# Banded attention joined to the MLP, with the tile scheduler choosing each engine's order

## The chip, the cores and the metric

The kernel runs on one core of one Trainium2 chip. The metric is the device time of the whole program in microseconds (us); most executions of a kernel agree within 0.3%. The core has five engines that matter here: PE (matrix products), ACT (table functions such as Exp, Ln and Sin), DVE (vector work), POOL (vector work, and the issue of DMAs that change the data type) and SP (other DMAs; ACT issues a few at the start). Each has its own queue of instructions. In the traces of this case an instruction waits behind those in front of it in its queue, also when its data are ready (POOL's copies between 95 and 120 us, below), and the waits between engines are read from semaphore events. The kernel is written in a tile language: the source gives the operations, and a scheduler decides in which order each engine's queue holds them, unless the source fixes it.

## The reference

```python
# 8 batches, 8 heads, 576 positions, head size 64; window 32; 8 global positions
scores = scale * q @ k.T
mask   = (|i - j| <= 32) | is_global[i] | is_global[j]
attn   = softmax(where(mask, scores, -1e9))
x      = (attn @ v), heads side by side              # 4608 tokens x 512
h      = x @ w_in                                    # 512 -> 2048
g      = h + sin(alpha * h)**2 / alpha
out    = g @ w_out                                   # 2048 -> 512
```

## The kernel before

The kernel before does dense attention for all batches, then the MLP. For each head it computes all 576 x 576 scores, transposed (keys on partitions), in six tiles of 96 keys, takes Exp on ACT, multiplies by a 0/1 mask on DVE, and multiplies by V with a column of ones appended, so that the softmax sum comes out as one more column.

```python
for b in range(B):
    if b == max(B - 2, 0):
        weight_prep()                # w_inp = w_in * alpha, w_outp = w_out / alpha, on DVE
    QS, KS, VS = ...                 # loads
    for hp in range(NHP):            # head pairs: transposes of q and k on PE, copies on DVE
        ...
        for t in range(2):
            for g in range(NKG):
                for gi in range(GK):
                    nc.tensor.matmul(out=scm[:, gi, :], lhsT=kTh[...], rhs=qTh[:, 0:SM], ...)
                    nc.tensor.matmul(out=sct[:, gi, :], lhsT=kTh[...], rhs=qTh[:, SM:S], ...)
                nc.scalar.activation(out=E[...], in_=scm[:, :, :], func=AF.Exp, scale=scale)
                nc.scalar.activation(out=E[...], in_=sct[:, :, :], func=AF.Exp, scale=scale)
                nc.vector.tensor_tensor(out=E[...], in0=E[...], in1=MASK[...], op=ALU.mult)
            ...                      # avq = E.T @ [V, 1]: 30 small matmuls; reciprocal, multiply on DVE
for tci in range(NCHUNK):            # 9 chunks of 512 tokens
    for nt in range(NT):             # 16: h2 = w_inp.T @ xT; Sb = Sin(h2) on ACT;
        ...                          # S2 = Sb*Sb and H2b = h2 + S2 on DVE
    ...                              # ops = H2b.T @ w_outp: 4 x 16 matmuls; copy on ACT; store
# (cut: set-up of the mask, transposes back, stores)
```

The softmax here doesn't subtract the row's maximum and nothing guards it: scores larger than these inputs give would overflow.

## Time and profile before

| | us |
|---|---|
| time, median | 733.14 |
| start, PE nearly idle | 0 to 81 |
| dense attention | 81 to about 471 |
| MLP, 28.2 us a chunk | about 475 to 732 |

Part 1 of the page (busy time of each engine and its share of the span), three rows of part 2 (busy share in 40 slices of the span, in tenths; PEclk is the clock granted to PE) and the first line of part 4 (the chain of work that ended last, by engine):

```profile
PE 642.0 (88%) x4360; PEld 352.6 (48%) x4384; DVE 412.0 (56%) x893; ACT 341.7 (47%) x566; POOL 107.7 (15%) x144
PE   0000699999999999999999999999999999999997
DMA  9999264918993999559968000001101001001001
PEclk9999999999999999999999999999999999999999
PE 83%; issue 6%; DVE 3%; POOL 3%; DMA 2%; ACT 2%; DVEq 0%; ACTq 0%; POOLq 0%
```

While the DMA engines bring in the first batch and the weights (DMA 9 in slices 1 to 4), PE does nothing for four slices; then it is full to the end, at full clock, and it makes up 83% of the chain. So PE sets the time, and the start stands in front of it. The costliest groups, part 5 (line, engine, operation, output<-inputs, shapes, count, busy us and mean ns of one, idle time before it and what ended it):

```profile
L259 PE MATMUL scm<-qT,kT 64*96 64x512 bf16 x384 | 202.2, 646 | 2.0 <-ACT E L273 0.9
L273 ACT ACTIVATE E<-scm 96x1024 bf16<-96x1024 f32 x192 | 195.8, 1020 | 41.1 <-PE scm L259 35.8
L285 DVE TENSOR_TENSOR E<-E,MASK 96x1152 bf16<-96x1152 bf16 x192 | 143.2, 747 | 24.9 <-ACT E L279 24.7
L297 PE MATMUL avq<-VS,E 96*128 96x65 bf16 (+1 forms) x1920 | 143.3, 245 | 1.1 <-DVE E L285 0.8
```

The first and last of these, 345 us of PE's 642, are dense scores and dense products with V. Three rows of the timeline of before matter for the argument, an early piece of DVE's work and the only two loads of function tables on ACT (start, duration, engine, line, and in brackets the idle time before and what ended it):

```profile
13.86 2.29 DVE L183 TENSOR_TENSOR w_inp<-wtmp,alphaB 128x2048 bf16<-128x2048 f32 x1 [3.75 <-DMA wtmp<-in_moe_w_in_dram]
...
81.55 1.28 ACT L273 ACT_TABLE_LOAD   x1 [81.55 <-PE sct L266]
...
474.77 1.28 ACT L369 ACT_TABLE_LOAD   x1 [3.72 <-issue]
```

The two loads bring in Exp's table and Sin's, each in 1.28 us. The first row shows DVE scaling `w_inp` at 14 us, although the source asks for it only before the seventh batch: the scheduler takes whatever is ready, from far ahead in the source.

### The profile page before, as it was taken

Reading aid. Unit: us, or ns where it says so; the run is one execution under the profiler, and the core shown is the slowest. Engines: PE = TensorE matmul, PEld = TensorE weight load, DVE = VectorE, ACT = ScalarE, POOL = GpSimd, SP = SyncE. Lnnn points to the kernel's source line nnn. Section 1 sums busy time; section 2 is a strip of 40 time slices with the busy share of each in tenths; the row PEclk is TensorE's granted clock in tenths of the full one; section 3 lists DMA queues with packets and bytes.
Section 4 is the critical chain, followed back from the end, with each engine's and each line's share of the span. In section 5 each row is a group of like instructions: output and inputs, shape, how many; then the busy total and the mean of one; then the engine's idle time right before and its main releaser. Section 6 shows DMA issues by size and latency. Waiting matters only on the chain.

```text
span 732.5 us, 10762 instructions
## 1 busy us (share of the span) xinstructions
PE 642.0 (88%) x4360; PEld 352.6 (48%) x4384; DVE 412.0 (56%) x893; ACT 341.7 (47%) x566; POOL 107.7 (15%) x144
## 2 busy tenths in 40 slices
PE   0000699999999999999999999999999999999997
PEld 0000356555665656565656666544444444444443
DVE  2466355555565655555555565594483573673762
ACT  0000465655565655555555565553353353353442
POOL 5167040122140131221500000000000000000000
PEclk9999999999999999999999999999999999999999
DMA  9999264918993999559968000001101001001001
GB/s 244 294 46 122 5 41 27 34 12 55 33 61 21 23 62 33 33 34 34 66 19 15 1 1 1 1 1 57 44 16 58 30 29 57 30 30 57 29 31 57
DMA packets 122529, 33.74 MB, mean 46 GB/s; under 512 B 115184, under 2 KB 115184, under 8 KB 121840
## 3 DMA queue, kind: packets, MB, share of 16 engines
q0 software_dynamic: 112256, 14.16, 49.3%
q1 hardware_dynamic: 10224, 18.89, 7.2%
q8 instruction: 34, 0.56, 0.3%
q14 instruction: 15, 0.12, 0.1%
HBM read 37.77 MB, written 9.44 MB: 64 GB/s over the span
## 4 chain that ended last, share of the span: by engine, by line
PE 83%; issue 6%; DVE 3%; POOL 3%; DMA 2%; ACT 2%; DVEq 0%; ACTq 0%; POOLq 0%
PE scm L259 21%; PE avq L297 17%; PE ops L383 17%; PE psx L237 5%; PE sct L266 5%; PE xps L329 2%; DMA QS<-in_q_dram 2%; DVE H2b L374 1%; ACT E L273 1%; POOL VS L79 1%; ACT Sb L369 1%; PE xps L335 1%; DVE Cq L111 1%; POOL KS L72 0%; POOL QS L72 0%
## 5 line engine op out<-in xcount | busy, mean ns | idle before, releaser
L273 ACT ACTIVATE E<-scm 96x1024 bf16<-96x1024 f32 x192 | 195.8, 1020 | 41.1 <-PE scm L259 35.8
L259 PE MATMUL scm<-qT,kT 64*96 64x512 bf16 x384 | 202.2, 646 | 2.0 <-ACT E L273 0.9
L285 DVE TENSOR_TENSOR E<-E,MASK 96x1152 bf16<-96x1152 bf16 x192 | 143.2, 747 | 24.9 <-ACT E L279 24.7
L297 PE MATMUL avq<-VS,E 96*128 96x65 bf16 (+1 forms) x1920 | 143.3, 245 | 1.1 <-DVE E L285 0.8
L297 PEld LDWEIGHTS <-E 96*128 96x128 bf16 (+1 forms) x1920 | 116.5, 135 | 53.1 <-issue 16.1
L383 PE MATMUL ops<-w_outp,H2b 128*128 128x512 bf16 x565 | 139.1, 379 | 0.6
L279 ACT ACTIVATE E<-sct 96x128 bf16<-96x128 f32 x192 | 51.8, 270 | 114.8 <-PE sct L266 114.4
L361 PEld LDWEIGHTS <-w_inp 128*128 128x128 bf16 x576 | 56.1, 98 | 74.3 <-issue 10.5
L383 PEld LDWEIGHTS <-H2b 128*128 128x128 bf16 x576 | 55.5, 98 | 68.8 <-DVE H2b L374 5.1
L266 PEld LDWEIGHTS <-kT 64*96 64x96 bf16 x384 | 58.4, 181 | 35.7 <-issue 26.7
L266 PE MATMUL sct<-qT,kT 64*96 64x64 bf16 x384 | 66.8, 264 | 0.0
L259 PEld LDWEIGHTS <-kT 64*96 64x96 bf16 x384 | 58.1, 173 | 15.3 <-issue 3.0
L391 ACT COPY osb<-ops 128x512 f32<-128x512 f32 x36 | 21.1, 585 | 84.3 <-PE ops L383 84.3
L237 PE MATMUL psx<-identb,QS 96*128 96x96 bf16 x192 | 21.9, 277 | 43.0 <-POOL identb masks.py:199 43.0
L237 PE MATMUL psx<-identb,KS 96*128 96x96 bf16 x192 | 26.2, 276 | 36.0 <-DVE qT L242 36.0
L305 DVE RECIPROCAL rec<-avq 128x4 f32<-128x4 f32 x64 | 11.7, 183 | 78.6 <-PE avq L297 78.6
L72 POOL DMA_DIRECT2D QS<-in_q_dram x48 | 36.9, 777 | 79.3 <-PE psx L237 78.5
L237 PEld LDWEIGHTS <-QS 96*128 96x128 bf16 x192 | 14.7, 133 | 57.2 <-issue 48.7
L237 PEld LDWEIGHTS <-KS 96*128 96x128 bf16 x192 | 15.4, 130 | 50.6 <-issue 50.6
L72 POOL DMA_DIRECT2D KS<-in_k_dram x48 | 36.9, 775 | 17.2 <-PE psx L237 15.1
L273 ACT ACT_TABLE_LOAD x1 | 1.3, 1283 | 81.5 <-PE sct L266 81.5
L242 DVE COPY kT<-psx 128x576 bf16<-128x576 bf16 x32 | 14.6, 455 | 33.0 <-PE psx L237 33.0
(614 smaller groups left out, 592.7 us busy)
## 6 DMA issues: line engine op xcount, KB each, us to landing
out_dram<-osb SPq DMA_DIRECT2D x36, 256.0 KB, 2.0
QS<-in_q_dram POOLq DMA_DIRECT2D x48, 96.0 KB, 3.6
KS<-in_k_dram POOLq DMA_DIRECT2D x48, 96.0 KB, 3.8
VS<-in_v_dram POOLq DMA_DIRECT2D x8, 576.0 KB, 11.1
wtmp<-in_moe_w_in_dram SPq DMA_DIRECT2D x4, 1024.0 KB, 8.4
alphaB<-in_moe_alpha_dram SPq DMA_DIRECT2D x1, 1024.0 KB, 5.8
wtmp_4073<-in_moe_w_out_dram SPq DMA_DIRECT2D x1, 1024.0 KB, 12.2
wtmp_4079<-in_moe_w_out_dram SPq DMA_DIRECT2D x1, 1024.0 KB, 10.4
```

The lines of the kernel that those rows point to most:

```text
L72: nc.gpsimd.dma_start(out=dstS[:, jt, :, :], in_=src[b, :, jt * KW : (jt + 1) * KW, :].rearrange("h p d -> p h d"),)
L237: nc.tensor.transpose(out=psx[:, jt * KW : (jt + 1) * KW], in_=srcS[:, jt, 2 * hp : 2 * hp + 2, :], identity=identb[0:KW, 0:KW],)
L259: nc.tensor.matmul(out=scm[:, gi, :], lhsT=kTh[:, k0 : k0 + KW], rhs=qTh[:, 0:SM], start=True, stop=True,)
L266: nc.tensor.matmul(out=sct[:, gi, :], lhsT=kTh[:, k0 : k0 + KW], rhs=qTh[:, SM:S], start=True, stop=True,)
L273: nc.scalar.activation(out=E[:, g * GK : (g + 1) * GK, 0:SM], in_=scm[:, :, :], func=AF.Exp, scale=scale,)
L279: nc.scalar.activation(out=E[:, g * GK : (g + 1) * GK, SM:S], in_=sct[:, :, :], func=AF.Exp, scale=scale,)
L285: nc.vector.tensor_tensor(out=E[:, g * GK : (g + 1) * GK, :], in0=E[:, g * GK : (g + 1) * GK, :], in1=MASK[0:KW, g * GK : (g + 1) * GK, :] ...
L297: nc.tensor.matmul(out=avq[0:qrows, qb, :], lhsT=E[:, kt, qs0 : qs0 + qrows], rhs=VS[:, hh * NKT + kt, :], start=(kt == 0), stop=(kt == NK ...
L329: nc.tensor.transpose(out=xps[:, qs0 : qs0 + QB], in_=xnp[:, qb, :], identity=identb[:, :],)
L361: nc.tensor.matmul(out=h2[:, :tn], lhsT=w_inp[:, c, nt * P : (nt + 1) * P], rhs=xT[:, c, t0 : t0 + tn], start=(c == 0), stop=(c == CT - 1),)
L383: nc.tensor.matmul(out=ops[:tsn, :], lhsT=H2b[:, nt, ts0 : ts0 + tsn], rhs=w_outp[:, nt, :], start=(nt == 0), stop=(nt == NT - 1),)
L391: nc.scalar.copy(out=osb[:tsn, :], in_=ops[:tsn, :])
```

## The change

The intent has three parts. First, only the band and the global rows and columns are computed: for 48 queries the keys are a window of 112 rows plus the 8 global ones, 120 of 128 partitions. A *unit* is one head pair and every second group of 48 queries; 8 units make a batch. Second, batch p's attention is emitted between matmuls of the MLP's second product for chunk p-1, and the first product of chunk p follows, so that PE has work while ACT and DVE do the softmax. Third, softmax's division is done on ACT as Exp(-Ln(den)). Work is also moved to POOL: 11 of the 16 squares of a chunk, half of `w_inp`'s scaling and all of `w_outp`'s.

```diff
+    MASK = const.tile([P, 2, NU, QC], BF, name="MASK")   # band and global rows
+    psA = tc.tile_pool(name="psA", bufs=1, space=PSUM)   # Sp, num, den, h2, ops, Kps: one buffer each
+    def stage_Q(b, hp, par):
+        Sp = psA.tile([P, 2, CH], F32, name="Sp")
+        for u in range(NU):                              # 6 matmuls, 112 columns each
+            nc.tensor.matmul(out=Sp[...], lhsT=kTw[hp][:, par, u, :], rhs=qBD[hp][:, par, u, :, :], ...)
+        nc.scalar.activation(out=E[:], in_=Sp[:, :, 0:EW], func=AF.Exp, scale=scale)
+        nc.vector.tensor_tensor(out=Ev, in0=Ev, in1=MASK[...], op=ALU.mult)
+    def stage_V(b, hp, par, E, xTb, gn, gd):
+        ...                                              # den = ones.T @ E (2), num = V.T @ E (6 matmuls)
+        nc.scalar.activation(out=lnd[:], in_=den[:], func=AF.Ln)
+        nc.scalar.activation(out=rec[:], in_=lnd[:], func=AF.Exp, scale=-1.0)
+        ...                                              # xTb = num * rec (2), gn = sum of num (2) on DVE
+        nc.vector.tensor_reduce(out=gd[:, par, hp, :], in_=den[:, :, QB:QC]..., op=ALU.add)
+    def stage_G(b, xTb, gn, gd):                         # global rows: 4 small DVE operations, then
+        for j in range(NG):
+            nc.gpsimd.tensor_copy(out=xTb[:, :, bass.ds(pregs[j], 1)], in_=xg[:, :, j : j + 1])
+        nc.vector.tensor_copy(out=xT[:, :, b * S : (b + 1) * S], in_=xTb[:])
+    # attention(b), before its first unit:
+                    nc.scalar.preload_act_table_set("natural_log_exp_and_others")
+    # first product of the MLP, squares shared between POOL and DVE:
+                nc.scalar.activation(out=Sb[:, 0:n, :], in_=h2[:], func=AF.Sin)
+                nc.gpsimd.tensor_tensor(out=S2[:, 0, :], in0=Sb[:, 0, :], in1=Sb[:, 0, :], op=ALU.mult)
+                if n == 2:
+                    nc.vector.tensor_tensor(out=S2[:, 1, :], in0=Sb[:, 1, :], in1=Sb[:, 1, :], op=ALU.mult)
+    # weights: w_inp half on DVE, half on POOL; w_outp on POOL
-    # (cut: dense scores, dense mask, the MLP as a phase of its own)
```

Nothing in the new source fixes the order on an engine. In particular the preload of the table set that holds both Ln and Exp has no data that it waits for.

## The prediction

> **What bounds the kernel now.** The busy table gives PE 642 of 732.5 us (88%), DVE 56%, ACT 47%, POOL 15%; the chain of waits is 83% PE. The timeline shows three stretches: about 81 us in which PE does nothing (loads, mask building), 390 us of dense attention (12.1 us per head pair, PE full), 257 us of MLP (28.2 us per chunk, PE full). Phases do not overlap; granted clock is 1.0.
>
> **What the change removes.** Dense scores become bands; most of the 202 us of scm and 143 us of avq matmuls goes. In the trace 26 avq matmuls with fresh weights take 1.68 us, 65 ns each, so a new unit (head pair, parity) costs 12 x 65 ns + 2 x 0.14 us, about 1.06 us; 64 units 68 us, transposes about 25 us. With the unchanged MLP (about 250 us) PE needs some 345 us. Estimates from the trace's shapes: ACT 225 us, DVE about 310 us, POOL 230 us. PE is no longer the sole limit.
>
> **What it adds and moves.** PSUM tiles Sp, num, den have one buffer each, so units run as a chain: matmuls 0.7 us, Ln 0.44, Exp 0.44 (from 96x1024 in 1.02, 96x128 in 0.27), two DVE multiplies 0.9 (128x256 took 0.42), three reduces 0.5, semaphore gaps 0.4: 3.4 us a unit, 27 us a batch, against 25 us of PE work there including the overlapped second MLP matmul. Then about 5 us of global rows and 18 us for the first MLP matmul. POOL squares are part of that: the Trainium skill, "GPSIMD Engine Reference", section 3.1, has tensor_tensor at 4497 ns for 128x2048; I estimate about 1.2 us for 512, 11 a chunk, equal to PE's 13.7 us. No trace shows it yet. Period about 53 us.
>
> **The scheduler.** In the trace of before, DVE scales weights at 14 us although the program asks for that at batch 6: order is chosen by readiness, far ahead. The preload of the combined Ln/Exp table has no data to wait for, so I expect all of them hoisted to the start. The Trainium skill, "ScalarE: Activation LUTs", section "Table sets", says one set holds both Ln and Exp; after Sin has evicted it, I expect separate Exp and Ln sets to be loaded in turn, two loads a unit. The trace has a load at 1.28 us (two of them, agreeing with that page's 1283 ns). Both sit in the unit's chain: 3.4 becomes 5.8 us, and the period about 71 us. I give this two chances in three.
>
> **Sum.** Start 50, batch 0 about 32, first MLP 18, seven periods, tail 45. Without thrashing 516 us, with it 642 us. Point 590, range 470 to 690. Faster 0.90, within 2% 0.04, slower 0.06. The removed PE work lies wholly on today's critical path.
>
> **What would show it.** ACT table loads: about 120 (thrash) or about 18. PE busy near 350 us, with its idle time waiting on DVE (num, den released) in attention and on POOL or DVE in the MLP. First score matmul near 50 us. POOL squares about 1.2 us.
>
> **What would make it wrong.** The scheduler keeps preloads in place (then about 500). Exp of the next batch mixed among Sins gives still more loads. POOL or DMA bound: q, k, v packets kept the DMA about 80% busy for 48 us a batch, some 39 us a batch, below my period but not by much. Weight loads hoisted ahead of batch 0's inputs delay the start.

## The result, and the profile after

| | before | after |
|---|---|---|
| time, median us | 733.14 | 646.64 |
| ratio | | 0.8823 (0.8803 to 0.8843) |
| PE / ACT / DVE / POOL busy, us | 642 / 342 / 412 / 108 | 395 / 362 / 347 / 305 |
| table loads on ACT | 2 | 129 |

A ratio here is always the mean time of one kernel's fast runs over that of the kernel before in the same rounds, so it is not quite the ratio of the medians quoted beside it. The same rows of the page as before:

```profile
PE 394.8 (61%) x2397; PEld 197.3 (31%) x2440; DVE 346.7 (54%) x702; ACT 362.1 (56%) x456; POOL 305.3 (47%) x451
PE   0153300485659665875486659764875587649997
ACT  0042100248944995499548954797479747974331
PEclk9995555598989788988999888889899989998999
ACT 25%; issue 24%; PE 20%; POOL 17%; DVE 9%; DMA 4%; POOLq 1%; DVEq 0%; ACTq 0%
```

PE is no longer full, and ACT has the largest share of the chain. The row of ACT beats in 9s and 4s: one beat is one batch. In slices 6 and 7 PE does nothing, and from slice 4 to 8 its clock is granted at half. What ACT does in the dense parts, from the groups of ACT's instructions:

```profile
L378 ACT ACT_TABLE_LOAD x56 | 71.8, 1283 | 1.0
L380 ACT ACT_TABLE_LOAD x45 | 57.7, 1283 | 0.8
L349 ACT ACTIVATE E<-Sp 128x672 bf16<-128x672 f32 x64 | 46.4, 725 | 30.5 <-PE Sp L342 30.3
L380 ACT ACTIVATE rec<-lnd 128x336 f32<-128x336 f32 x64 | 30.8, 481 | 0.7
L378 ACT ACTIVATE lnd<-den 128x336 f32<-128x336 f32 x64 | 28.8, 450 | 15.3 <-PE den L363 14.7
L349 ACT ACT_TABLE_LOAD x18 | 23.1, 1283 | 0.3
L546 ACT ACT_TABLE_LOAD x8 | 10.3, 1283 | 103.8 <-PE h_852 L539 53.6 <-PE h_1420 L539 7.8 <-PE h_3692 L539 7.8
L435 ACT ACT_TABLE_LOAD x2 | 2.6, 1283 | 22.0 <-DMA gN_158<-in_v_dram 21.2 <-PEq L648 0.8
```

Line 349 is the scores' Exp, 378 the Ln, 380 the reciprocal's Exp, 546 Sin, 435 the preload. The 119 loads in front of Ln and Exp take 153 us, more than those functions (106 us). Of eight preloads in the source two are left in the program. The timeline of ACT shows where they went (two rows from the start, then a stretch of batch 1):

```profile
0.81 1.28 ACT L435 ACT_TABLE_LOAD   x1 [0.81 <-PEq L648]
23.30 1.28 ACT L435 ACT_TABLE_LOAD   x1 [21.21 <-DMA gN_158<-in_v_dram]
...
142.39 1.28 ACT L349 ACT_TABLE_LOAD   x1
143.68 0.73 ACT L349 ACTIVATE E<-Sp 128x672 bf16<-128x672 f32 x1
145.13 0.73 ACT L349 ACTIVATE E<-Sp 128x672 bf16<-128x672 f32 x1 [0.71 <-PE Sp L342]
145.87 1.28 ACT L378 ACT_TABLE_LOAD   x1
147.17 0.45 ACT L378 ACTIVATE lnd<-den 128x336 f32<-128x336 f32 x1
147.64 1.28 ACT L380 ACT_TABLE_LOAD   x1
148.93 0.48 ACT L380 ACTIVATE rec<-lnd 128x336 f32<-128x336 f32 x1
```

Both preloads start in the first 24 us, before any Exp. From Sin's first use on, each unit loads one set for Ln and another for Exp. By the starts of the eight Ln's of this batch (147.17 to 179.46) a unit takes 4.6 us. The two halves of a period, from the view of busy time by stretch (stretch, its length, then busy us and count of PE, PEld, DVE, ACT and POOL, granted clock, DMA, GB/s):

```profile
142.40:190.40 48.00, 27.23 (x193) 14.86 (x197) 25.03 (x65) 36.68 (x45) 18.40 (x39) 0.90 0.52 56
190.40:210.00 19.60, 18.32 (x84) 7.62 (x85) 12.91 (x17) 9.65 (x12) 12.64 (x13) 0.90 0.58 51
```

In the attention half ACT is busy 37 of 48 us and is the busiest engine; in the MLP half PE is, with 18.3 of 19.6.

The idle stretch near the start has another cause. Rows of the timeline of POOL and DVE between 82 and 121 us, the kernel after:

```profile
82.03 4.61 DVE L410 TENSOR_TENSOR gs<-gn 128x32 f32<-128x32 f32 x1
...
88.05 6.19 POOL L482 TENSOR_SCALAR w_outp<-wtmp,recipT 128x512 bf16<-128x512 f32 x4
...
95.08 0.21 POOL L413 COPY xTb<-xg 128x4 bf16 x1
...
111.94 6.18 POOL L482 TENSOR_SCALAR w_outp<-wtmp,recipT 128x512 bf16<-128x512 f32 x4
...
119.92 0.21 POOL L413 COPY xTb<-xg 128x4 bf16 x1
...
120.16 0.76 DVE L416 COPY xT<-xTb 128x2304 bf16<-128x2304 bf16 x1 [33.30 <-POOL xTb L413]
```

The eight tiny copies of batch 0's global rows (line 413) stand in POOL's queue among the scalings of `w_outp` (line 482, four in 6.2 us), so the copy into `xT` that the MLP waits for comes after DVE had sat idle for 33 us. Seven of batch 0's eight units were done at 69 us, and the first Sin starts at 124. The eighth unit ended only at 82 us: its matmuls with V stood on PE behind batch 1's transposes of K, and these waited for their loads between 68 and 80 us. The first row is a DVE operation on 128x32 values that took 4.61 us; its seven others took 0.19.

The time can be laid out as I did in the prediction:

| stretch | predicted, with thrashing (two loads a unit) | after |
|---|---|---|
| to the end of the first MLP half | 100 | 142.4 |
| seven periods | 7 x 71 = 497 | 7 x 65.8 = 461 |
| tail | 45 | 42 |
| sum | 642 | 645 |

The end of the first MLP half is the first Exp load at 142.39; seven periods are the time from the first Sin load (122.9) to the eighth (583.5). So the total is right partly by luck: two errors, +42 and -36 us, cancel. Inside a period errors cancel too. Eight units of 4.6 us are 37 us of the attention half of 48.0, so 11 us stand around the units, where I had put 5; that hid part of the error in the unit, for which I had 5.8.

### The profile page after: what moved, and what is told of

It is laid out like the page before. It is cut to its first block, busy times and chain, and to the rows that moved or that the text cites. A ratio compares the mean times of both kernels' runs of the same rounds, so it can differ in the third digit from the quotient of the medians.

```text
span 645.4 us, 7446 instructions
## 1 busy us (share of the span) xinstructions
PE 394.8 (61%) x2397; PEld 197.3 (31%) x2440; DVE 346.7 (54%) x702; ACT 362.1 (56%) x456; POOL 305.3 (47%) x451
## 4 chain that ended last, share of the span: by engine, by line
ACT 25%; issue 24%; PE 20%; POOL 17%; DVE 9%; DMA 4%; POOLq 1%; DVEq 0%; ACTq 0%
ACT L378 8%; PE ops L575 5%; DVE H2b L524 4%; DMA VW_92<-in_v_dram 4%; POOL w_outp L482 4%; PE Sp L539 4%; ACT lnd L378 3%; ACT E L349 3%; PE num L539 3%; ACT L380 3%; ACT Sb L546 3%; ACT rec L380 2%; POOL xTb L413 2%; PE Sp L342 2%; POOL KS L103 1%
## 5 line engine op out<-in xcount | busy, mean ns | idle before, releaser
L575 PE MATMUL ops<-w_outp,H2b 128*128 128x512 bf16 x411 | 116.3, 405 | 2.3 <-DVE H2b L524 1.2
L385 DVE TENSOR_TENSOR xTb<-num,rec 64x288 bf16<-64x288 f32 x128 | 58.2, 454 | 82.6 <-ACT rec L380 60.3
L378 ACT ACT_TABLE_LOAD x56 | 71.8, 1283 | 1.0
L546 ACT ACT_TABLE_LOAD x8 | 10.3, 1283 | 103.8 <-PE h_852 L539 53.6
L539 PE MATMUL num<-xT,w_inp 128*128 128x512 bf16 x209 | 63.1, 444 | 3.4 <-DVE H2b L524 3.1
L349 ACT ACTIVATE E<-Sp 128x672 bf16<-128x672 f32 x64 | 46.4, 725 | 30.5 <-PE Sp L342 30.3
L380 ACT ACT_TABLE_LOAD x45 | 57.7, 1283 | 0.8
L546 ACT ACTIVATE Sb<-num 128x1024 bf16<-128x1024 f32 x27 | 27.6, 1022 | 30.1 <-PE num L539 26.1
L351 DVE TENSOR_TENSOR E<-E,MASK 128x672 bf16<-128x672 bf16 x64 | 31.9, 507 | 14.1 <-ACT E L349 13.1
L110 POOL DMA_DIRECT2D VW_92<-in_v_dram x28 | 21.2, 763 | 34.7 <-PE num L371 29.9
L378 ACT ACTIVATE lnd<-den 128x336 f32<-128x336 f32 x64 | 28.8, 450 | 15.3 <-PE den L363 14.7
L539 PE MATMUL Sp<-xT,w_inp 128*128 128x512 bf16 x140 | 34.0, 379 | 0.6 <-DVE H2b L524 0.3
L363 PE MATMUL den<-E,ones_77 128*128 128x336 bf16 x64 | 22.0, 343 | 18.9 <-DVE gd L398 16.5
L371 PE MATMUL num<-E,VW_91 128*128 128x112 bf16 x192 | 19.2, 242 | 23.2 <-DVE gn L393 22.9
```

What stands on the lines that cost most here:

```text
L349: nc.scalar.activation(out=E[:], in_=Sp[:, :, 0:EW], func=AF.Exp, scale=scale)
L351: nc.vector.tensor_tensor(out=Ev, in0=Ev, in1=MASK[:, par, :, None, :].to_broadcast([P, NU, 2, QC]), op=ALU.mult,)
L378: nc.scalar.activation(out=lnd[:], in_=den[:], func=AF.Ln)
L380: nc.scalar.activation(out=rec[:], in_=lnd[:], func=AF.Exp, scale=-1.0)
L385: nc.vector.tensor_tensor(out=xv[:, :, :, par, :], in0=numv[pr, :, :, t, 0:QB], in1=rec[pr, :, 0:QB].rearrange("p (a u) c -> p a u c", a=2 ...
L539: nc.tensor.matmul(out=h2[:, k_, :], lhsT=w_inp[:, ci, (nt + k_) * P : (nt + k_ + 1) * P], rhs=xT[:, ci, t0 : t0 + CH], start=(ci == 0), s ...
```

## The experiments

All ten kernels gave correct results.

### The preload tied to its place

Theory A: the loads are in the chain of each unit. Theory B: `num` and `den`, which have one buffer each and are freed by DVE, set the pace, and the loads fill time in which ACT would be idle anyway. The edit adds order edges on ACT and no wait:

```diff
-                    nc.scalar.preload_act_table_set("natural_log_exp_and_others")
+                    pre = nc.scalar.preload_act_table_set("natural_log_exp_and_others").ins
+                    act["pre"] = pre
+                    if act.get("sin") is not None:
+                        after(pre, act["sin"])      # order edge: behind the last Sin so far
...
+        after(<the scores' Exp>, act["pre"])        # order edge: every Exp behind its preload
```

> Only order edges on ACT are added: each table preload after the last Sin of the chunk before it, each score Exp after its batch's preload. The program then holds 16 table loads in place of 129. Theory A (the two loads a unit stand in the chain through Ln and Exp): the seven attention stretches fall from about 48 us to 28 to 35, the period from 66 to 47 to 53, the time to 515 to 555 us. Theory B (ACT is busy but the single-buffered num and den, freed by DVE, set the pace, so the loads fill idle time): period stays above 62, time above 615 us.

Measured: 526.76 us, ratio 0.7178 (0.7161 to 0.7196), 16 loads. Two stretches as above, the attention half and the MLP half of one period:

```profile
143.30:173.90 30.60, 24.71 (x198) 13.09 (x197) 24.65 (x65) 16.03 (x30) 18.78 (x39) 0.94 0.83 83
173.90:193.50 19.60, 17.95 (x86) 7.55 (x85) 12.39 (x17) 9.62 (x12) 12.59 (x13) 0.92 0.54 58
```

The attention half fell from 48.0 to 30.6 us, with the same work on DVE (25 us) and ACT's 36.7 us down to 16.0; the MLP half did not change. Ln's of batch 1 start at 146.82 to 163.30, 2.35 us a unit. In the profiled runs 113 loads fewer are worth 645.4 - 527.0 = 118.4 us, 1.05 us each, of the 1.28 us that one takes. Theory A holds; theory B falls.

### Source order on ACT alone, and on every engine

Is anything else lost by the scheduler's order? Two kernels fix the order of the source from the first batch on, one on ACT only, the other on all engines.

```diff
+    with tc.manual_schedule(engines={Activation}):   # second kernel: tc.manual_schedule()
         global_v(0)
         ...                                          # the rest of the program, indented
```

> ACT alone keeps the order of the source text; all other engines are still ordered by the scheduler. Also 16 table loads. If the loads are all that the scheduler's ACT order costs, this equals the tied kernel within 2%. If the scheduler's mixing of score Exp, Ln and reciprocal Exp is itself worth something, this is over 2% slower than the tied kernel.

> Every engine keeps the order of the source text from the first batch on. Theory A alone (only the table loads matter): within 2% of the tied kernel. Theory C (the scheduler also costs time elsewhere: batch 1's transposes on PE wait for loads ahead of batch 0's last unit, POOL's weight scaling stands ahead of batch 0's global rows): 15 to 50 us below the tied kernel, first Sin before 105 us in place of 123. Rival: fixed order blocks in-order engines and is slower than the tied kernel.

Measured: ACT alone 529.62 us, ratio 0.7221 (0.7209 to 0.7233), 0.6% over the tied kernel and so inside the 2%: on ACT the loads are all that the scheduler's order costs. It is also a second order of ACT's instructions with the same 16 loads, so what the tied kernel saved is the loads and not a lucky order. Every engine: 575.35 us, ratio 0.7854 (0.7840 to 0.7867), 9% slower than the tied kernel. Theory C had a point for the start only: the first Sin came at 106.4 in place of 126.1, but periods grew from 49 to about 58 us. Over the periods the scheduler's order is better than the source's. The waits of the all-engines kernel (who waited for whom: total us, times, longest) name a reason:

```profile
PE den L363 <- DVE gd L398: 82.2, 56, 7.7
ACT lnd L378 <- PE den L363: 101.2, 59, 8.8
```

`den` has one buffer, and the last to read it is the reduction `gd`, which the source puts at the end of the unit. In the changed kernel the scheduler moved it up, in most units to right after Ln (for 47 of the 64 reductions DVE's wait ended with Ln).

### Source order with one statement moved

```diff
+        nc.vector.tensor_reduce(out=gd[...], in_=den[...], op=ALU.add)   # now before num * rec
         numv = num[...]
         ...
-        nc.vector.tensor_reduce(out=gd[...], in_=den[...], op=ALU.add)
```

> Source order on every engine as in the source-order run (575 us), with one statement moved: the reduction of den to the global rows comes first after the matmuls, not last. If the source-order kernel is slower than the tied one because den is freed only at the end of each unit (PE waited 82 us on that reduction), the attention stretch falls from 36 to about 31 us and the time by 25 to 45 us, to 530 to 550. If the loss lies in the MLP or elsewhere, the time falls by under 10 us.

Measured: 537.02 us, ratio 0.7327 (0.7307 to 0.7348), on another chip. The wait that named the reason is now:

```profile
PE den L363 <- DVE gd L381: 14.0, 10, 8.6
```

One statement's place is worth 38 us, as expected; the attention half went from 36 to 30.3 us (Exp at 129.7, next Sin at 160.0), as short as in the tied kernel. What is left of the loss lies in the MLP half, 22.9 us (to 182.9) against 19.6; its cause was not looked for. The moved statement also explains the size of my estimate: 3.4 us a unit is about what the source order gives (Ln's from 134.00 to 156.86 in the all-engines kernel, 3.3 us a unit), while the scheduler reaches 2.35.

### The preload deleted

```diff
-                    nc.scalar.preload_act_table_set("natural_log_exp_and_others")
```

> The preload line is deleted from the changed kernel, nothing else; the program then holds 144 table loads. If the hoisted preloads help batch 0 alone, as I hold, batch 0 now also alternates between the sets and the time rises by at most 15 loads x 1.05 us, to 648 to 665, and batches 1 to 7 do not change (period 66 us). If the preloads did something for the later batches, the period rises by over 2 us and the time goes above 665.

Measured: 645.13 us, ratio 0.8802 (0.8776 to 0.8827), with 144 loads. Batches 1 to 7 did not change (Sin at 189.2 and 255.4, a period of 66 us), so in the changed kernel the eight preloads do nothing for them. My lower bound of 648 was missed: the 15 loads more in batch 0 cost nothing that the runs can tell, since batch 0 ends in the idle stretch anyway. In these runs a load cost time only where its chain ended last.

### The output weights off POOL

```diff
-                    nc.gpsimd.tensor_scalar(out=w_outp[:, t, :], ...)
+                    nc.vector.tensor_scalar(out=w_outp[:, t, :], ...)
```

> The 16 scalings of the output weights move from POOL (1.56 us each, 24.7 us) to DVE, nothing else; 129 table loads stay. If POOL's queue is what holds batch 0's global rows back until 120 us, the first Sin comes at 95 to 102 us in place of 123 and the time falls by 20 to 28 us, to 618 to 627. If the hole has another cause (loads, w_inp), the time falls by under 8 us.

On the changed kernel: 626.24 us, ratio 0.8543 (0.8529 to 0.8558), 20 us less, the first Sin at 106.3 in place of 124.2. That is the low end of what I expected in us, and the first Sin is some 4 us later than expected: the copies still stood behind DMA issues in POOL's queue. The row of the copy into `xT`, now at 102.29 us in place of 120.16:

```profile
102.29 0.76 DVE L416 COPY xT<-xTb 128x2304 bf16<-128x2304 bf16 x1 [11.99 <-POOL xTb L413]
```

> The tied preloads and the output weights scaled on DVE, together. If the two costs are independent (loads in the seven later batches, POOL's queue in the first), the gains add: 527 less about 20, 504 to 510 us, 16 table loads. If the tied kernel already hides the hole, over 518.

Together with the tied preload: 509.63 us, ratio 0.6947 (0.6930 to 0.6965), 16 loads, 17 us below the tied kernel (526.76, on another chip). The two costs add, nearly in full.

### The rest of the start

```diff
-                eng = nc.vector if c < 2 else nc.gpsimd
+                eng = nc.vector
...
             tr = nc.tensor.transpose(out=Kps[...], in_=KS[...], ...)
+            after(tr.ins, act["num", b - 1])     # order edge on PE: behind the batch before
```

> As the last, and also the input weights all on DVE, and each batch's K transposes on PE held (order edge) behind the last num matmul of the batch before. Theory C (the rest of the hole at the start is order: PE's transposes waiting for loads ahead of batch 0's last unit, and POOL scaling weights ahead of the global rows): first Sin at 80 to 95 us in place of 105, time 480 to 500. Rival (the start is bound by loading q, k, v and weights): first Sin stays above 100, time above 502 us.

Measured: 501.67 us, ratio 0.6845 (0.6825 to 0.6864), the first Sin at 95.1 us. Both numbers lie on the edge between the two theories, and the run holds two edits at once, so it does not settle the rest of the start. The chain of waits in this stretch now names loads (the last chunk of V of a batch from 46.3 to 77.6 us, K from 78.6 to 85.9), which speaks for loading; that was not tested.

### The squares off POOL

```diff
-                nc.gpsimd.tensor_tensor(out=S2[:, 0, :], in0=Sb[:, 0, :], in1=Sb[:, 0, :], op=ALU.mult)
+                nc.vector.tensor_tensor(out=S2[:, 0, :], in0=Sb[:, 0, :], in1=Sb[:, 0, :], op=ALU.mult)
    # second kernel: nc.scalar.activation(out=S2[:, 0, :], in_=Sb[:, 0, :], func=AF.Square)
```

> On the fastest kernel so far (501.7 us): the squares that POOL takes (11 a chunk, 1.04 to 1.3 us each) go to DVE, nothing else. My prediction held that POOL's squares are part of what makes the MLP half 19.6 us against 13.7 of PE work. In that trace DVE's own square takes 0.95 to 1.1 us beside POOL's and took 0.42 in the kernel before. If POOL beside DVE costs time, DVE squares return to about 0.42 us, the MLP half falls below 18.5 us and the time to 480 to 494. If PE (busy 17.8 of 20 us there) sets the half, the time stays within 1%.

> The same squares go to ACT instead, which is idle half of the MLP half. Loads stay at 16. If taking the squares off POOL helps by freeing DVE, 476 to 492 us, and no slower than the variant with all squares on DVE; if PE sets the half, within 1% of 501.7; if ACT's longer queue delays Sin and with it PE, slower.

Measured: all on DVE 485.25 us, ratio 0.6603 (0.6579 to 0.6627); on ACT 491.92 us, ratio 0.6696 (0.6676 to 0.6716). The groups of squares (count, busy us and mean ns) in the kernel of the last section, where POOL takes its part:

```profile
L565 POOL TENSOR_TENSOR S<-Sb 128x512 bf16<-128x512 bf16 x99 | 108.7, 1115 | 101.8 <-ACT Sb L563 96.7 <-DVE H2b L541 5.0
L569 DVE TENSOR_TENSOR S<-Sb 128x512 bf16<-128x512 bf16 x45 | 38.6, 857 | 11.2 <-ACT Sb L563 11.1
```

The same groups in the kernel with all squares on DVE:

```profile
L565 DVE TENSOR_TENSOR S<-Sb 128x512 bf16<-128x512 bf16 x99 | 41.6, 420 | 41.2 <-ACT Sb L563 40.9
L569 DVE TENSOR_TENSOR S<-Sb 128x512 bf16<-128x512 bf16 x45 | 18.8, 418 | 0.0
```

DVE's own 45 squares took 857 ns each on average beside POOL and 418 ns without it (422 where ACT took POOL's part). POOL's 99 squares cost 109 us on POOL and 42 us on DVE, and DVE's other 45 became 20 us cheaper. The time is inside what I expected, but the place is not: the stretch from the first Sin to the next Exp did not shrink (18.6 and 19.5 us before, 19.4 and 19.7 after, with PE busy 18.9 of 19.4), and it was the attention half that shrank, from 31 to 28 us (116.6 to 145.4, and 164.8 to 192.4). PE loaded weights more often in the MLP half (102 times against 92): six transposes of K and about four matmuls of the first product had moved into it, while the second product's share of the two halves was the same (51 and 13 weight loads in both kernels). Why the attention half became 3 us shorter was not tested. That ACT would be no slower a place than DVE was wrong by 1.4%; why was not tested. How much is POOL's slowness and how much DVE's stretching beside it, these two runs do not separate. The kernel with all squares on DVE is the fastest, 34% below the kernel before and, by the two ratios, 25% below the changed one.

## Why the prediction was right or wrong

- **Point, range and direction: right.** 590 predicted, 470 to 690; 646.64 measured. The thrashing case alone summed to 642.
- **Preloads hoisted, two loads a unit, in the chain: right, and shown.** Two preloads remain, both started before 24 us; 129 loads against about 120; deleting the source line changes nothing from batch 1 on; tying it takes 118 us off. The Trainium skill, "ScalarE: Activation LUTs", section "Table sets", which the prediction rests on, says that one set serves both functions; the tied kernel agrees, with one load a batch for Exp and Ln together. A load took 1283 ns in every one of the 129, as that page's section "What ACT_TABLE_LOAD costs" has it.
- **"3.4 us a unit", "3.4 becomes 5.8": mis-sized.** Measured 2.35 without thrashing (tied) and 4.6 with it (changed). The difference, 2.3 us, is close to the predicted 2.4. The 3.4 failed because I laid the unit out in source order, with the reduction of `den` at its end; source order gives 3.3, and moving that one statement saved 38 us in all. The 5 us for global rows, the rest of the attention half, was too small by 6 to 7 us in both kernels (11.1 in the changed, 11.8 in the tied). I had expected order chosen by readiness to hurt, and did not see that it would also help.
- **"Start 50, batch 0 about 32, first MLP 18": wrong by 42 us.** The first score Exp was even earlier than I said (33.9 us), but I missed POOL's queue. I listed POOL's total and never asked what stands in front of the eight small copies that end batch 0. Taking `w_outp` off POOL gave back 20 us, 17 on the tied kernel. The other 22 us or so are not explained by an experiment; the trace shows batch 0's last unit waiting until 80 us behind transposes whose loads were late.
- **"Without thrashing 516": near.** The tied kernel takes 527, again as a sum of a longer start and shorter periods (49 in place of 53).
- **PE busy near 350: low.** It was 395, with a mean granted clock of 0.87; the tied kernel, at 0.90, has 373, and the fastest, at 0.92, has 365 (some 40 of 2440 matmul records are missing from the first and the last of these traces). That the clock is the reason was not tested by itself.
- **PE's idle time "waiting on DVE (num, den released)" in attention: right in part.** PE waited 46 us for DVE before `num` and 16 before `den`, but also 38 us for ACT's Exp before `Sp`, which I had not named. POOL's total was low: 305 us against my 230.
- **POOL's squares about 1.2 us: right**, 1.04 to 1.28. The estimate came from the Trainium skill, "GPSIMD Engine Reference", section 3.1, and that page's own size, 128x2048, took 4.50 us on POOL here. Their full cost was not: DVE beside them doubled.
- **DMA as the limit: not in the steady part** of the changed kernel, where the DMA column of the two halves says 0.52 and 0.58. In the fastest kernel it says 1.15 and 1.23 in two attention halves; whether loads limit that kernel was not tested. Whether DMA is the limit at the start is open.

## What to carry to other kernels

An instruction that only changes an engine's state (a table preload) has no data that holds it in place, so a scheduler that works by readiness may issue it long before it is of use; give it an order edge, and count the loads in the compiled program before anything is timed. Fixing all orders is not the remedy: here the scheduler's order (with the preloads tied) beat the source's by 9%, and one late reader of a single-buffered PSUM tile explained most of that. For each small operation that ends a stage, ask what else stands in its engine's queue; here POOL's was worth 20 us.

## What the Trainium skill lacked or had wrong

- "ScalarE: Activation LUTs", section "What ACT_TABLE_LOAD costs", puts a switch at about 2.66 us, 1283 ns of load and about 1380 ns of drain. Here an Ln ended at 147.62, the load ran from 147.64 to 148.92, and the next Exp started at 148.93: 1.31 us in all. Taking loads away was worth 1.05 us each.
- The same page, in its rules, says to use the set that holds both Exp and Ln, "1 load, not 2". It does not say that after a third function the two are served from separate sets again unless the combined one is asked for in the right place: 129 loads against 16, and 118 us. With no preload at all it was so from the first batch on: 144 loads.
- "GPSIMD Engine Reference", section 8, names contention with DVE for SBUF, and that section gives no size; another page of the skill takes the matter up. Here DVE's 128x512 bf16 square took 857 ns on average beside POOL's squares and 418 ns alone, and a 128x32 DVE operation took 4605 ns while POOL ran a 128x2048 one of 4.50 us, against 192 ns otherwise.
- "TensorE: Matmul & The Clock Gate", part 1, on the clock that falls to half when PE idles: the runs agree (0.50 granted from 87 to 123 us). After a gap of 3.6 us at 188 us the first matmuls of a chunk, at a granted clock of 0.50, took 0.63 us in place of 0.38. Nothing was wrong there.
